# A spectral filter with a mixer on one core: first group of batch 0 closed by selection matmuls, and a new order of the opening loads

## The chip, the cores and the metric

The kernel runs on one core of a Trainium2 chip. The metric is the device time of one execution in microseconds. A core has five engines, each with its own queue that is worked in order: TensorE (PE in the profile; its weight loads are PEld), VectorE (DVE), ScalarE (ACT), GpSimd (POOL) and SyncE (SP). Transfers are issued by SP, by ScalarE and, where the type changes on the way, by GpSimd.

## The reference

```python
def _attn_ref(x, filt_r, filt_i):              # x: (8, 3136, 256)
    X = np.fft.rfft(x, axis=1)
    Y = X * (filt_r + 1j * filt_i)[None, :, :]
    return np.fft.irfft(Y, n=x.shape[1], axis=1).astype(np.float32)

def _moe_ref(x, U, V, w_ch1, w_ch2):           # U: (3136, 32), V: (32, 3136)
    h = x.transpose(0, 2, 1) @ U @ V
    u = x + h.transpose(0, 2, 1)
    ch = np.maximum(u @ w_ch1, 0.0) @ w_ch2    # 256 -> 1024 -> 256
    return (u + ch).astype(np.float32)
```

The second function is applied to the output of the first. All inputs and outputs are float32; the kernel computes in float16 with float32 sums.

## The kernel before

The sequence of 3136 is split as 64 x 49, and the transform is done by matmuls in four stages, for each of eight batches.

- Stage 1 (`st1`, lines 260 to 290): a transform over the 64, with its twiddle factors folded into the matrix `wf`. Thirteen units per batch; the result goes to a DRAM scratch, `ct1`. Batch 0 takes another way: `turned` (line 295) gives the result turned round, and it stays on chip (`cm`, which lies in the tile `fc`).
- Stage 2 and the filter: a transform over the 49 (`stage2`, matmuls of lines 348 to 352), and a product with the filter. For batch 0 (`mid_first`, line 354) half a block at a time is multiplied once (L400 on VectorE, L397 on GpSimd after a copy by ScalarE, L395), with four stage-2 matmuls for a block of two halves and four in stage 3. For later batches (`plan_mid`, line 610) a block of four frequencies has two stage-2 matmuls (`two`), three products (`mul`, L628, L630, L632, on VectorE, or on GpSimd for the blocks that are `pooled`) and a sum on GpSimd (L634). These need turned and negated copies of the filter tiles, which `make_fa` (line 541) makes: L543 on ScalarE, L544 and L545 on VectorE.
- Stage 3 (`stage3`, L344): back over the 49; the result is copied to `esb` (L326) and stored to a second DRAM scratch, `ct2` (L329). `low_rank` (L416) and `low_rank_end` (L424, L426) take the product with U from the same tiles.
- Groups. Each batch's output is made in six groups of 512 tokens and a small one of 128 for two batches together. `load_e2` (L438, by SP) brings a group's 64 rows from `ct2`, `put_h` adds 32 rows for the low-rank part, and `stage4` (L477, copied to `ut` by L482) is the transform back over the 64 with the matrix `sv`, whose last 32 rows are V. Then `mm1` (L488) and its relu (L492) make one of eight parts of the hidden layer; this is a step. `mm2_part` (L521) of the group before, with `residual` (L497), runs in the same step, and the result leaves by L529 and L536.

The order of instructions on every engine is the order in which the program writes them. The opening is written out (lines 552 to 578): `u_hat`, `turned`, `mid_first`, stage 1 of batch 1, then stage 4 of the first group. After it, a loop over groups and steps issues what two lists hold for each step: `early` ahead of mm1 and `plan` behind mm2. `plan_mid`, `plan_st1` and `plan_rest` fill them, so that stages 1 to 3 of batch b run in the steps of batch b-1 (and stage 1 of b+1 before them). Each instruction waits for its data by semaphores, with all behind it in its queue. GpSimd is not tied to the steps: it goes on as soon as the data of its next instruction are there. `load_x` (two issues per tile, L170) uses four tile buffers; the tile rings and PSUM banks (`bank`) set further waits.

## Time and profile before

| | |
|---|---|
| median of 6 runs | 556.64 us (555.33 to 559.0) |
| the profiled execution's own time | 555.66 us |
| its span | 553.9 us |
| mean granted TensorE clock | 0.986 |
| busy: PE, ACT, DVE, POOL | 517.1, 390.9, 352.9, 282.4 us |
| first mm1 (L488) | 57.33 us |
| last store issued (L513) | 550.09 us |

The page lists busy time by engine, then the span in 40 slices of 13.8 us with the busy share in tenths, the granted clock and the DMA load. Other views of the same execution give the busy time of each engine in a chosen stretch, what each engine waited for in a stretch, and single instructions in order of time. Times are from the start of the span. A wait is put down to what came last.

### The profile page before, as it was taken

The numbers are of one execution on the slowest core, as the hardware profiler recorded it, in microseconds if no ns is written. First come the engines' busy times: TensorE is split into PE (matmuls) and PEld (weight loads), VectorE is DVE, ScalarE is ACT, GpSimd is POOL, SyncE is SP. The second block draws the span as 40 slices with busy tenths as digits, with TensorE's granted clock in tenths as the row PEclk, the third lists the DMA queues.
The fourth block names the chain that finished last, engine by engine and source line by source line (L and its number), as shares of the span: only waits on it lengthen the run. The fifth ranks groups of instructions, "written<-read, shape, count | busy, mean of one in ns | idle before, by whom it ended". The sixth has DMA issues, their size and how long they took to land.

```text
span 553.9 us, 11638 instructions
## 1 busy us (share of the span) xinstructions
PE 517.1 (93%) x4491; PEld 375.4 (68%) x4491; DVE 352.9 (64%) x409; ACT 390.9 (71%) x684; POOL 282.4 (51%) x194
## 2 busy tenths in 40 slices
PE   5986698987999999999999999999999999999996
PEld 3733366764767777677776777777776777777775
DVE  6774864754746785758746785768646887643332
ACT  8576778764777688677777788668767677765663
POOL 5787379931893165815683185807563287300000
PEclk9999799997999999999999999999999999999999
DMA  9998888885669468775879469865654554333212
GB/s 196 160 177 184 227 172 212 184 198 158 164 175 252 129 172 209 161 200 145 196 213 219 123 173 234 168 201 152 178 171 126 141 164 121 106 113 115 96 78 87
DMA packets 85433, 92.06 MB, mean 166 GB/s; under 512 B 6742, under 2 KB 69417, under 8 KB 85377
## 3 DMA queue, kind: packets, MB, share of 16 engines
q1 hardware_dynamic: 67968, 75.12, 45.6%
q0 software_dynamic: 16960, 15.91, 19.2%
q8 instruction: 35, 0.57, 0.4%
q10 hardware_dynamic: 448, 0.28, 0.2%
q14 instruction: 22, 0.17, 0.1%
HBM read 57.42 MB, written 49.77 MB: 194 GB/s over the span
## 4 chain that ended last, share of the span: by engine, by line
PE 64%; POOL 5%; DVE 3%; ACT 1%; issue 1%; DMA 1%; ACTq 0%; POOLq 0%; DVEq 0%
PE psum L521 24%; PE psum L488 23%; PE psum L352 3%; PE psum L344 3%; PE psum L497 3%; PE psum L477 3%; PE psum L266 2%; POOL y L634 2%; DVE tb L632 1%; PE psum L416 1%; POOL x L170 1%; POOL tb L632 1%; POOL tb L630 1%; POOL ta L628 1%; DVE ut L482 1%
## 5 line engine op out<-in xcount | busy, mean ns | idle before, releaser
L492 ACT ACTIVATE hring<-psum 128x512 f16<-128x512 f32 (+1 forms) x416 | 237.6, 576 | 103.7 <-PE psum L488 102.4
L488 PE MATMUL psum<-ut,w1sb 128*128 128x512 f16 (+1 forms) x832 | 241.7, 372 | 3.5 <-ACT hring L492 1.7
L521 PE MATMUL psum<-w2sb,hring 128*128 128x256 f16 x1536 | 231.4, 274 | 0.0
L634 POOL TENSOR_TENSOR y<-ta,tb 128x1024 f16<-128x1024 f16 x56 | 120.5, 2159 | 160.8 <-DVE tb L632 129.3
L521 PEld LDWEIGHTS <-hring 128*128 128x128 f16 x1536 | 143.7, 98 | 62.8 <-issue 3.0
L482 DVE CAST ut<-psum 128x512 f16<-128x512 f32 x96 | 71.0, 740 | 107.6 <-PE psum L477 86.3
L488 PEld LDWEIGHTS <-w1sb 128*128 128x128 f16 x832 | 104.8, 145 | 26.3 <-issue 9.5
L529 DVE COPY och<-psum 128x512 f32<-128x512 f32 x96 | 66.1, 689 | 47.6 <-PE psum L497 46.2
L326 ACT CAST esb<-psum 98x512 f16<-98x512 f32 x128 | 74.7, 586 | 20.4 <-PE psum L344 14.3
L628 DVE TENSOR_TENSOR ta<-psum,fb 128x1024 f16<-128x1024 f32 x41 | 49.9, 1218 | 9.5 <-PE psum L352 8.5
L273 ACT CAST asb<-psum 128x512 f16<-128x512 f32 x78 | 45.7, 589 | 14.3 <-PE psum L266 13.2
L497 PE MATMUL psum<-idn,ut 128*128 128x128 f16 x392 | 54.0, 219 | 0.0
L477 PEld LDWEIGHTS <-e 96*128 96x128 f16 x768 | 35.7, 98 | 25.2 <-issue 9.8
L630 DVE TENSOR_TENSOR tb<-psum,fc 64x1024 f16<-64x1024 f32 x41 | 50.3, 1226 | 0.9
L632 DVE TENSOR_TENSOR tb<-psum,fc 64x1024 f16<-64x1024 f32 x41 | 49.9, 1218 | 0.8
L477 PE MATMUL psum<-sv,e 96*128 96x64 f16 x768 | 38.6, 193 | 6.1 <-DMA e<-ct 3.4
L344 PE MATMUL psum<-y,g 128*98 128x512 f16 x105 | 40.1, 382 | 2.7 <-POOL y L634 1.3
L497 PEld LDWEIGHTS <-ut 128*128 128x128 f16 x392 | 38.5, 98 | 4.9
L352 PE MATMUL psum<-a,w2t 98*128 98x512 f16 x113 | 34.7, 383 | 4.6 <-DMA a<-ct 3.6
L628 POOL TENSOR_TENSOR ta<-pc,fb 128x1024 f16<-128x1024 f16 x15 | 32.4, 2158 | 11.8 <-ACT pc L638 11.8
L266 PE MATMUL psum<-x,wf 128*128 128x256 f16 x168 | 31.6, 275 | 3.2 <-DVE asb L271 1.0
L630 POOL TENSOR_TENSOR tb<-pc,fc 64x1024 f16<-64x1024 f16 x15 | 31.8, 2123 | 1.2
(93 smaller groups left out, 370.3 us busy)
## 6 DMA issues: line engine op xcount, KB each, us to landing
out_dram<-och SPq DMA_DIRECT2D x47, 512.0 KB
ct<-esb SPq DMA_DIRECT2D x64, 196.0 KB
x<-in_x_dram POOLq DMA_DIRECT2D x48, 256.0 KB, 8.3
e<-ct SPq DMA_DIRECT2D x48, 256.0 KB
a<-ct SPq DMA_DIRECT2D x56, 196.0 KB
ct<-asb SPq DMA_DIRECT2D x42, 256.0 KB
...
```

The source lines that it names most:

```text
L326: nc.scalar.copy(esb[b, k][:, 2 * half:2 * half + 2, :].rearrange("p s d -> p (s d)"), pe[0:98])
L477: nc.tensor.matmul(pu[:, 64 * i:64 * i + 64], e2[b, c][:, i, 128 * dh:128 * dh + 128], sv[:, 64 * r:64 * r + 64], start=(i == 0), stop=Tru ...
L482: nc.vector.tensor_copy(o, v)
L488: nc.tensor.matmul(ph[:, 0:n], w1sb[:, dh, :, t], gr.ut[:, dh, 0:n], start=(dh == 0), stop=(dh == 1))
L492: nc.scalar.activation(h[:, 0:n], ph[:, 0:n], RELU)
L497: nc.tensor.matmul(o[:, dh * 128:dh * 128 + 128], gr.ut[:, dh, t0:t0 + n], idn, start=False, stop=(dh == 1), skip_group_check=True)
L521: nc.tensor.matmul(o, gr.h[tt][:, i * 128:(i + 1) * 128], w2sb[:, tt, :], start=(tt == 0), stop=False, skip_group_check=True)
L529: nc.vector.tensor_copy(gr.och[:, 2 * y:2 * y + 2, :].rearrange("p j d -> p (j d)"), gr.pc)
L628: eng.tensor_mul(ta, p, va)
L630: eng.tensor_mul(tb[0:64], p[64:128], vb[64:128])
L632: eng.tensor_mul(tb[64:128], p[0:64], vb[0:64])
L634: nc.gpsimd.tensor_add(ys[k], ta, tb)
```

## The change

- The opening. `wf` is loaded at half its size and spread out by two products with a column of zeros and ones on VectorE; U comes in float32 by SP; `u_hat` is done in pieces between the calls of `turned`; `cm` has a tile of its own. The first part of `sv` and `kr` are loaded after batch 0's first block, the rest of `sv` after its last; the filter's last slot is loaded after `w1`.
- `mid_first`: two turned blocks instead of four ahead of the first stage 2; only product 13 is on GpSimd; the parts of the low-rank product follow their blocks. Stage 4 of the first group reads from DRAM only what the first six blocks stored. What the last two blocks add is picked out of `esb` by 0/1 matrices (`sel`, `pick`, 64 small matmuls), copied once (`zs`) and multiplied with `s4x`; the low-rank part is a third product into the same bank.
- Batch 1. Only x tile 0 is loaded early; the other loads and the second weight stand behind product 13 on GpSimd, and the second weight is read in pieces of 512 numbers. Three units of stage 1 come ahead of the first mm1, ten in steps 0 to 7; its last three stores go out on GpSimd, behind eight copies of filter tiles there. Four of its eight blocks (0, 1, 6, 7) are multiplied once per half, as batch 0's are, the others later than before (steps 17 to 37 for their stage 2).
- The turned and negated filter copies are made in 24 pieces: eight copies on GpSimd after the loads, eight negations and four copies on VectorE in steps 5 to 13, four copies on GpSimd late in batch 0.
- Loads of x: batch 2 in steps 13 to 16, behind a one-element copy on GpSimd that reads the first stage-1 block of batch 1; batch 3 in steps 47 to 53 instead of with stage 1 of batch 2.
- The plans of batches 2 and 3 begin later, batch 2 with three blocks on GpSimd instead of two. Tiles of 128 rows become 113 rows. From step 98 on the plan is as before.

The diff, cut to its core:

```diff
+    sel = np.zeros((98, 4, 60))
+    s4x = np.zeros((128, 512))
+    for g in range(4):
+        for h in range(2):
+            for c in range(2):
+                sel[49 * c + 2 * g + h, g, 28 + 2 * h + c] = 1.0
+                n = 64 * (2 * g + h)
+                s4x[32 * g + 2 * h + c:32 * g + 32:4, n:n + 64] = s[48 + c:64:2, 2 * g + h]
+    wf = np.concatenate([wf.reshape(128, 25 * 64).astype(f16), pair.view(f16)], axis=1)
...
-    wf = cst.tile([128, 25, 128], F16, name="wf")
-    for c in range(4):
-        i = slice(8 * c, min(8 * c + 8, 25))
-        nc.sync.dma_start(wf[:, i], wf_d.rearrange("p (i m) -> p i m", m=128)[:, i])
+
+    usb = hflat[0:64, 0:2 * NR * RANK].bitcast(F32)
+    nc.sync.dma_start(usb, moe_U.rearrange("(q r) p -> q (r p)", q=NQ))
+    wfc = hflat[:, 6272:6272 + 1604]
+    nc.sync.dma_start(wfc, wf_d)
+    wf = cst.tile([128, 24, 128], F16, name="wf")
+    wl = cst.tile([64, 64], F16, name="wl")
...
+    cm = cst.tile([128, 7232], F16, name="cm")
+    nc.vector.memset(cm[:, 2 * SEQ:], 0.0)
...
+    for h in range(2):
+        nc.vector.tensor_scalar_mul(wf[:, :, 64 * h:64 * h + 64],
+                                    wfc[:, 0:1536].rearrange("p (i m) -> p i m", m=64),
+                                    wfc[:, 1600 + 2 * h:1602 + 2 * h].bitcast(F32))
+    nc.vector.tensor_copy(wl, wfc[0:64, 1536:1600])
+    tbs = [cst.tile([NZ, 4 * DM], F16, name=f"tb_{i}") for i in range(3)]
+    for t in tbs:
+        nc.vector.memset(t[32:64], 0.0)
...
-    w2sb = cst.tile([128, 8, DM], F16, name="w2sb")
-    vnat = hflat[64:96, 4704:4704 + SEQ]
+    w2sb = cst.tile([128, 4, 2 * DM + 16], F16, name="w2sb")
...
                 dst = asb[:, 2 * j:2 * j + 2, :].rearrange("p i d -> p (i d)")
-                if b == 1 and j % 2:
-                    nc.vector.tensor_copy(dst, pf)
-                else:
-                    nc.scalar.copy(dst, pf)
+                (nc.vector.tensor_copy if 4 * c + j in by else nc.scalar.copy)(dst, pf)
                 if j < 3:
                     yield
             for h in range(2):
-                nc.sync.dma_start(dram(ct1[b], (16 * c + h) * 64 * DM,
-                                       [[DM, 64], [128 * DM, 8], [1, DM]]), asb[64 * h:64 * h + 64])
-            if 1 < b < NB - 1 and c:
+                (nc.gpsimd if (b, c) == (1, 2) else nc.sync).dma_start(
+                    dram(ct1[b], (16 * c + h) * 64 * DM, [[DM, 64], [128 * DM, 8], [1, DM]]),
+                    asb[64 * h:64 * h + 64])
+            if 2 < b < NB - 1 and c:
                 load_x(b + 1, c - 1)
...
+    def make_fc(k, copy):
+        copy(fc[0:NR, 4 * k:4 * k + 4], fb[64:NZ, 4 * k:4 * k + 4])
+
+    def make_neg(k):
+        nc.vector.tensor_scalar_mul(fc[64:NZ, 4 * k:4 * k + 4], fb[64:NZ, 4 * k:4 * k + 4], -1.0)
+
+    def make_fa(k, copy):
+        copy(fa[64:NZ, 4 * k:4 * k + 4], fb[0:NR, 4 * k:4 * k + 4])
+        if k == 7:
+            nc.gpsimd.tensor_copy(fa[64:65, 31, :], fc[0:1, 31, :])
+            for p in (0, 64):
+                nc.gpsimd.memset(fc[p:p + 1, 31, :], 0.0)
+
...
+        def low_rank_part(k):
+            for i in range(4):
+                a = 4 * k + i
+                nc.tensor.matmul(ph[32 * i:32 * i + 32], uh[:, a, :], esb[0, k][:, i, :],
+                                 start=(k == 0), stop=(k == 7), skip_group_check=True)
+
+        whole = []
+        pu = [psum[:, 2 + dh, :] for dh in range(2)]
+        zp = psum[:, 0, 0:DM]
+
+        def pick(j):
+
+            for i in range(2):
+                sl = 2 * (j - 12) + i
+                for g in range(4):
+                    nc.tensor.matmul(zp[32 * g:32 * g + 32], sel[:, g, 28 - 4 * sl:60 - 4 * sl],
+                                     esb[0, j // 2][:, 2 * (j % 2) + i, :], start=(sl == 0),
+                                     stop=(sl == 7), skip_group_check=True)
 
         def do3(j, uv):
             pe = bank("e0")
             stage3(pe, [(uv[:, 0], 2, 4), (uv[:, 1], 3, 5)], j == 15)
-            out3(0, j // 2, j % 2, pe)
-
-        for k in range(4):
+            while whole and j > 3:
+                low_rank_part(whole.pop(0))
+            if j > 13:
+                pick(j - 2)
+            k = j // 2
+            out3(0, k, j % 2, pe)
+            if ndone[0, k] == 2:
+                whole.append(k)
+                if k == 0:
+                    nc.sync.dma_start(sv[0:64, 0:512], s4_d[:, 0:512])
+                    nc.sync.dma_start(kr, kr_d)
+                if k == 5:
+                    load_e2(0, 0, 48)
+                if k == 6:
+                    load_e2(0, 1, 48)
+                if k == 7:
+                    load_e2(0, 1, 64, 48)
+                    nc.sync.dma_start(sv[0:64, 512:], s4_d[:, 512:])
+                    load_e2(0, 2)
+                    load_e2(0, 6)
...
+
+        for k in range(2):
             turn_a2(k)
-        for c in range(4):
-            load_x(1, c)
-        nc.gpsimd.dma_start(w2sb, moe_w_ch2.rearrange("(cc t) e -> cc (t e)", t=8))
+        load_x(1, 0)
+        nc.gpsimd.tensor_copy(sv[64:96, :].rearrange("p (r q) -> p r q", q=NQ),
+                              vnat.rearrange("p (q r) -> p r q", q=64))
...
-            if j in (7, 9, 12, 14):
-                pc = sb.tile([128, 2, 2 * DM], F16, tag="pc", bufs=2, name="pc")
-                nc.scalar.copy(pc, pz)
-                uv = sb.tile([128, 2, 2 * DM], F16, tag="y", bufs=3, name="uv")
+            fin = free(fb, 0, NZ, 2 * j * DM, [[0, 2], [1, 2 * DM]])
+            uv = sb.tile([NZ, 2, 2 * DM], F16, tag="y" if j == 13 else "ta", bufs=3, name="uv")
+            if j == 13:
+                pc = sb.tile([NZ, 2, 2 * DM], F16, tag="pc", bufs=2, name="pc")
+                nc.scalar.copy(pc, pz[0:NZ])
                 nc.gpsimd.tensor_mul(uv, pc, fin)
             else:
-                uv = sb.tile([128, 2, 2 * DM], F16, tag="ta", bufs=3, name="uv")
-                nc.vector.tensor_mul(uv, pz, fin)
-            if j < 4:
-                turn_a2(j + 4)
+                nc.vector.tensor_mul(uv, pz[0:NZ], fin)
+            if j < 6:
+                turn_a2(j + 2)
             todo.append((j, uv))
-            if len(todo) > 3:
+            if j == 15:
+                todo = [todo[i] for i in (1, 0, 2)]
+            while len(todo) > 2 or todo and j == 15:
                 do3(*todo.pop(0))
-        while todo:
-            do3(*todo.pop(0))
-
-
-    h1 = {}
+        step1(1)
+        step1(1)
+        pick(14)
+        low_rank_part(7)
+        pick(15)
+        h1[0] = hp = sb.tile([128, DM], F16, tag="hp", bufs=1, name="hp")
+        nc.vector.tensor_copy(hp, ph)
+        zs = sb.tile([128, DM], F16, tag="zs", bufs=1, name="zs")
+        nc.scalar.copy(zs, zp)
+        keep_warm(2, psum[:, 7, :])
+        low_rank_end(0)
+        gr = groups[0]
+        gr.ut = sb.tile([128, 2, 512], F16, tag="ut", bufs=3, name="ut")
+        for dh in range(2):
+            for i in range(8):
+                nc.tensor.matmul(pu[dh][:, 64 * i:64 * i + 64],
+                                 e2[0, 0][0:48, i, 128 * dh:128 * dh + 128],
+                                 sv[0:48, 64 * i:64 * i + 64], start=(i == 0), stop=False,
+                                 skip_group_check=True)
+        for dh in range(2):
+            nc.tensor.matmul(pu[dh], zs[:, 128 * dh:128 * dh + 128], s4x, start=False, stop=False,
+                             skip_group_check=True)
+        step1(1)
+        for dh in range(2):
+            nc.tensor.matmul(pu[dh], h1[0][64:96, 128 * dh:128 * dh + 128], sv[64:96, 0:512],
+                             start=False, stop=True, skip_group_check=True)
+            (nc.scalar.copy if dh else nc.vector.tensor_copy)(
+                gr.ut[:, dh, :].rearrange("p (j q s) -> p s j q", q=64, s=2),
+                pu[dh].rearrange("p (s j q) -> p s j q", s=2, q=64))
...
     keep_warm(10)
-    u_hat()
-    for c in range(4):
-        turned(c)
-        keep_warm(2)
-    nc.sync.dma_start(sv[0:64], s4_d)
-    nc.sync.dma_start(kr, kr_d)
+    turned(0, 0)
+    u_hat(0, 8)
+    keep_warm(2)
+    turned(0, 1)
+    u_hat(16)
+    keep_warm(2)
+    for c in (2, 3):
+        turned(0, c)
+    u_hat(24)
+    gens, a2q = {}, {}
+
+    def step1(b):
+        if b not in gens:
+            gens[b] = st1(b, (0, 3, 4, 5, 7, 8, 9, 11) if b == 1 else ())
+        next(gens[b])
+
     mid_first()
-    load_e2(0, 0)
-    load_e2(0, 1)
-    nc.gpsimd.tensor_copy(sv[64:96, :].rearrange("p (r q) -> p r q", q=NQ),
-                          vnat.rearrange("p (q r) -> p r q", q=64))
-    low_rank(0)
-    for n, _ in enumerate(st1(1)):
-        if n == 3:
-            low_rank_end(0)
-        if n == 6:
-            put_h(0, 0)
-    load_e2(0, 2)
-    load_e2(0, 6)
-    keep_warm(6)
-    stage4(groups[0], 0)
-    stage4(groups[0], 1)
-    for c in (1, 2, 6):
-        put_h(0, c)
-    make_fa(0)
-    make_fa(1)
+    keep_warm(3, psum[:, 7, :])
+    load_x(1, 1)
+    load_x(1, 3)
+    load_x(1, 2)
+    nc.gpsimd.dma_start(w2sb[:, :, 0:2 * DM], moe_w_ch2.rearrange("(cc i t) e -> cc i (t e)", i=4, t=2))
+    for k in (3, 2, 5, 4, 0, 1, 6, 7):
+        make_fc(k, nc.gpsimd.tensor_copy)
+    put_h(0, 1)
...
+        def two_q(k, half):
+            box[k, half] = [psum[:, 5:7, :]]
+            for f in range(2):
+                stage2(psum[:, 5 + f], w2t[:, 128 * f:128 * f + 128],
+                       w2t[:, 256 + 128 * f:384 + 128 * f],
+                       a2[k][:, 2 * half * DM:2 * half * DM + 2 * DM], (k, half) == (7, 1))
+
+        def mul_q(k, half):
+            uv = sb.tile([NZ, 2, 2 * DM], F16, tag="ta", bufs=3, name="uv")
+            nc.vector.tensor_mul(uv, box[k, half][0][0:NZ],
+                                 free(fb, 0, NZ, (4 * k + 2 * half) * DM, [[0, 2], [1, 2 * DM]]))
+            box[k, half].append(uv)
+
+        def three_q(k, half):
+            uv = box[k, half][1]
+            pe = bank("e")
+            stage3(pe, [(uv[:, 0], 2, 4), (uv[:, 1], 3, 5)], (k, half) == (7, 1))
+            out3(b, k, half, pe)
+
+        end = 0
+        if b == 1:
+
+            for k, q in ((0, 11), (3, 11), (1, 11), (5, 11), (2, 17), (4, 20), (6, 22), (7, 25)):
+                at(q, fetch, k)
+            for k, q, d in ((3, 17, 26), (5, 21, 31), (2, 23, 33), (4, 28, 37)):
+                at(q, two, k)
+                if k % 2:
+                    early[q + 1].append((pooled, (k,)))
+                else:
+                    w = q
+                    for i in range(3):
+                        w += 1
+                        while not ok_dve(w):
+                            w += 1
+                        early[w].append((mul, (k, i, nc.vector)))
+                for half in range(2):
+                    at(d + half, three, k, half)
+            for k, qs in ((0, (15, 16)), (1, (19, 20)), (6, (33, 34)), (7, (36, 37))):
+                for half, q in enumerate(qs):
+                    at(q, two_q, k, half)
+                    early[q + 1].append((mul_q, (k, half)))
+                    at(q + (3 if k == 7 else 2), three_q, k, half)
+            return 40
...
         for k in range(3):
-            at(later(s, -lead), fetch, k)
-        end = 0
+            at(later(s, -5 if b == 2 else -9), fetch, k)
         for k in range(8):
...
-                s = later(s, 3 if b > 1 else 1)
+                s = later(s, 3)
...
-                d = max(later(s, 5), end)
+                d = max(later(s, 3 if (b, k) == (2, 7) else 5), end)
...
     for c in range(3, 6):
         at(8 * c - 14, load_e2, 0, c)
-    at(1, make_fa, 2)
-    at(3, make_fa, 3)
-
-    def x_after(b):
-
-        for c in range(4):
-            load_x(b, c, groups[0].h[3] if c == 0 else None)
-
-    at(4, x_after, 2)
+    for n, c in ((7, 2), (8, 6), (9, 0)):
+        at(n, put_h, 0, c)
+    for n in (0, 0, 1, 1, 2, 3, 4, 5, 6, 7):
+        at(n, step1, 1)
+    at(13, lambda: load_x(2, 0, a2q[0][0:1, 0:1]))
+    for c in range(4):
+        if c:
+            at(13 + c, load_x, 2, c)
+        at((47, 49, 51, 53)[c], load_x, 3, c)
+    for n, k in ((5, 0), (5, 1), (7, 2), (8, 3), (8, 4), (9, 5), (11, 6), (11, 7)):
+        at(n, make_neg, k)
+    for n, k in ((12, 2), (12, 3), (13, 4), (13, 5)):
+        at(n, make_fa, k, nc.vector.tensor_copy)
+    for n, k in ((34, 0), (35, 1), (40, 6), (41, 7)):
+        at(n, make_fa, k, nc.gpsimd.tensor_copy)
     for b in range(1, NB):
         if b == 2:
-            plan_st1(b, 12, (0, 1, 3, 4, 5, 7))
+            plan_st1(b, 18, (0, 3, 4, 5, 7))
         elif b > 2:
-            plan_st1(b, later(start[b - 1], -60))
-        m = later(start[b - 1], (5, -9, -12)[min(b, 3) - 1])
-        z = plan_mid(b, m, (2, 5) if b > 1 else (1, 3, 5))
+            plan_st1(b, later(start[b - 1], -46 if b == 3 else -60), (0, 3, 4, 5, 7) if b == 3 else (0, 4, 7))
+        m = later(start[b - 1], (16, -4, -12)[min(b, 3) - 1])
+        z = plan_mid(b, m, (2, 5) if b > 2 else (1, 3, 5))
...
                 f(*a)
             mm1(gr, t)
-            if n + 1 < len(groups) and t in ((2, 6) if n != 5 else (6, 7)):
-                stage4(groups[n + 1], t // 4 if n != 5 else t - 6)
+            turns = {0: (5, 6), 5: (6, 7)}.get(n, (2, 6))
+            if n + 1 < len(groups) and t in turns:
```

## The prediction

> **What bounds the kernel now.** I read the busy rows and slices of the page first, then the busy time by stretch, then TensorE's waits by window, then single rows in time order. A "step" is one mm1 (line 488) with its relu (L492). The relu rows in time order put step 0 at 58.7, 16 at 80.6, 40 at 116.6, 48 at 133.3 and 98 at 190.6 us; each step's number and work follow from the plan lists.
>
> The page:
>
> ```profile
> PE 517.1 (93%) x4491; PEld 375.4 (68%) x4491; DVE 352.9 (64%) x409; ACT 390.9 (71%) x684; POOL 282.4 (51%) x194
> PE   5986698987999999999999999999999999999996
> PEclk9999799997999999999999999999999999999999
> ```
>
> TensorE is the bound from slice 10 on. The first ten slices hold nearly all that is lost, and the two low clock digits lie there. By stretch (PE, PEld, DVE, ACT, POOL, clock, DMA share, GB/s):
>
> ```profile
> 46.00:57.30 11.30, 6.96 (x80) 4.50 (x80) 5.70 (x8) 7.73 (x13) 5.94 (x1) 1.00 0.73 191
> 60.20:63.60 3.40, 1.54 (x6) 0.68 (x6) 3.01 (x6) 3.40 (x4) 0.65 (x2) 1.00 0.68 175
> 63.60:70.50 6.90, 5.14 (x22) 2.54 (x22) 6.14 (x10) 3.50 (x6) 4.31 (x7) 0.51 0.94 214
> ...
> 125.10:128.50 3.40, 0.72 (x13) 0.71 (x14) 0.22 (x1) 0.00 (x0) 0.00 (x0) 1.00 0.82 222
> 128.50:135.30 6.80, 5.96 (x31) 3.54 (x29) 4.94 (x6) 2.52 (x5) 1.57 (x1) 0.50 0.43 128
> ```
>
> Two thin stretches, each followed by 6.8 us at half clock. TensorE's waits from 57 to 75 us and from 110 to 140 us name the causes:
>
> ```profile
> PE psum L352 <- DMA a<-ct: 2.2, 1, 2.2
> PE psum L488 <- ACT hring L492: 1.7, 2, 1.5
> ```
> ```profile
> PE psum L477 <- DMA e<-ct: 3.4, 1, 3.4
> PE psum L352 <- DMA a<-ct: 1.4, 1, 1.4
> ```
>
> The last is the hand-off to batch 1: its final ct store is issued at 117.80, its e load only at 123.88, and stage 4 starts at 127.78. The rows that price the opening:
>
> ```profile
> 24.79 3.48 DVE L400 TENSOR_TENSOR uv<-psum,fb 128x1024 f16<-128x1024 f32 x3
> 41.16 5.85 SPq L329 DMA_DIRECT2D ct<-esb  x4
> 44.98 6.96 POOL L562 COPY sv<-hring 32x3136 f16<-32x3136 f16 x1
> 52.09 1.10 SPq L438 DMA_DIRECT2D e<-ct  x2
> ```
>
> Products of batch 0 start at 24.79, its last ct store is issued near 47.0, the e loads wait for it until 52.09, and the first mm1 comes at 57.33.
>
> **The change, stage by stage.** From step 98 on both plans are the same, so all is decided before 190.6.
>
> *A, up to the first mm1 (57.3 before).* The DMA share is 1.03 in the first 20 us, at 194 GB/s, and the x landings pace the four turned(c), at 13.55, 16.0, 18.7 and 20.4. Ahead of them half of wf (-399 KB) and sv with kr (-416 KB) go away; U in f32 and sel with s4x come in (+196, +174). Net -445 KB, at 194 GB/s 2.3 us. The expansion of wf and the f32 U copies (DVE, some 3 us, by L243's 1.48 and L544's 0.69 for 2048) hide under x. Two turn-backs instead of four before the first stage 2 give 0.5 more: first product at 22.0. The loop is DVE's: 15 products x 1.23 + one copy 0.69 = 19.1, to 41.1 (before 12 on DVE with 4 on GpSimd: also 19.1). Last esb 43.5, against 46.7.
>
> Then the gain: before, 10.7 us of store, load and stage 4 follow. After, columns 0 to 47 of group 0 need only ct stores 0 to 5, and the rest comes from the selection matmuls (64 of L416's form, 0.03 each, 2.0 in all, three of four picks between waits for esb). esb 11 is done at 39.8; store to landing 2.4 (180.53 to 182.89), load 3.1 (62.28 to 65.36): e at 45.3; sixteen matmuls 0.4, s4x 0.43, a stage-1 unit 0.22, h part 0.2, ut 0.74: first mm1 at 47.3. The other branch (hp 0.37, kr 0.27, h1 0.36, h part, ut, from 43.8) ends at 46.3 and is covered. **A: -10.0.** If store and load take what they take before (5.1 and 3.9), 50.8.
>
> *B, first mm1 to step 16 (23.3 before).* make_fa leaves ScalarE (L543, four of 1.89) and becomes eight GpSimd copies of 49x1024, with negs and copies on DVE at 0.35 each (half of L544's 0.69). Ten stage-1 units (0.22 on TensorE each, 2.1 in all; copies 0.58 to 0.69, eight of twelve on DVE) enter steps 0 to 7. Moved behind GpSimd's product (41.8): five x(1) issues at 0.65 and w2sb 0.57, so issued by 45.8; then the copies; then three ct_1 stores, which a(1,0) on SP needs. Some 2 MB of x, w2sb and e take 10.5 us at 190 GB/s; the 2 KB pieces I cost at nothing, as w2 is due only at step 8. Stage 4 of group 1 at step 5 needs sv's rest and e_1, near 52.5 (store of k=7 at 44, landed 47 to 48, then loads): about 1 us of wait. Step 8 at 56.5; seven steps at 1.05: step 15 ends at 64. asb of c=2 is ready at 57.2, stores 1.3, landing 3.5, load 3.1: a(1,0) at 65.2, wait 1.2; step 16 at 66.7. x(2) waits on GpSimd behind a(1,0), and behind it queue batch 1's pooled products; stage 1 of batch 2 begins at step 19, 5 us later, so it is just covered. **B: 19.4, -3.9.**
>
> That holds while GpSimd is free by 57.2, at up to 1.43 us per copy. The trace has one copy on GpSimd: L562, 3136 elements with a strided input in 6.96, so 2.2 ns each, 2.3 per copy and 18.2 for eight. The Trainium skill, "GPSIMD Engine Reference", section 4.1 with 3.1, says two inputs cost twice VectorE but one input runs at about line rate (1.03 cycles of 1.2 GHz per element): an estimate of 0.88 per copy, 7 for eight; it also calls GpSimd the wrong engine for plain elementwise work. By the row GpSimd is free at 64.0, by the page at 52.8. The trace agrees for two inputs (L634 2.1 ns per element); a contiguous single input is not in it. The row's input is strided, so I take 1.2 (9.6), nearer the page; both ends stay in the range.
>
> The wait at step 5 could also drop the clock. "TensorE: Matmul & The Clock Gate" (HAM oscillation) speaks of idle gaps over about 3.4 us. The trace is harsher: 1.54 busy in 3.40 was enough at 60.2, with a longest gap of 2.2. By the page a 1 us wait costs nothing more; by the row a thin stretch costs 3.4 (half of 6.8). At 52 the neighbours are busy some 65%, so I charge none here.
>
> *C, steps 16 to 40 (36.0 before).* TensorE content from spacings of starts (mm1 pair 0.43, four mm2 0.43, residual pair 0.11, stage 4 0.21, stage-2 pair 0.43, stage-3 half 0.21, stage-1 unit 0.22): before 20.6+1.3+1.3+2.0+2.6+2.9 = 30.7, so 5.3 of waits, with GpSimd busy 37.25 of 38 us from 72 to 110. After: 20.6+1.3+1.3+2.9+3.0+1.7+3.4+1.7 = 35.9, as four blocks of batch 1 use four matmuls for two; GpSimd falls to about 26 of 38 and I leave half the waits. **C: 38.5, +2.5.**
>
> *D, steps 40 to 48 (16.7 before).* Content 9.7. The chain from the last stage 3 to stage 4 at step 46: esb 0.6, issue 0.3, store 2.4 to 6.1, load 3.1 to 3.9, thus 6.4 to 10.9 against 7.3 of steps. x of batch 3 has later steps, but GpSimd is not held by steps: its first half tile goes once the fa copies are through, near step 40, and three a(2) loads stand ahead of the store on SP. So I take 9.5, a wait of 2.2, and half of a 3.4 clock loss: **D: 13.7, -3.0.**
>
> *E, steps 48 to 98 (57.3 before).* One stage-2 block and four stage-1 units fewer are behind us: 0.43+0.88, rounded to **+1.5**. Batch 2 now ends at step 92 for stage 4 at 98, 7.8 us: just enough for 6.4 to 7.
>
> Sum: -10.0-3.9+2.5-3.0+1.5 = **-12.9**: span 541.0 for 553.9. The profiled run took 555.66, 1.8 over its span; the median is 556.64. So **543.7**.
>
> **The rivals.**
> - *No stall at all* (0.19): A's other branch sets mm1 (-1), no wait for a(1,0) (-1.2), D at its content plus 0.5 (-3.5): 538. For it: from 140 to 300 us TensorE's waits add up to only 1.9 us. Against: by the bytes counted in B the DMA engines stay near full until past 60 us.
> - *The first group is not closed sooner than its e load* (0.09): store 5.1, load 3.9 as before: mm1 at 50.8, 547.2. For it: rows 41.16 and 52.09; against: x(1) is no longer in flight at 40.
> - *GpSimd copies at the strided row's 2.3* (0.11): a(1,0) at 71.9, 6.7 later, and a half-clock spell 3.4: 553.8.
> - *Slower* (0.08): the same queue at over 2.6 us per copy. It decides when 8 x (c - 1.43) and the 3.4 exceed 12.9: from c = 2.6 us; at 3.2 it gives 561. For it: DVE's copies and negs run beside these on the same tiles; against: no GpSimd group with two inputs has a mean over 2.16.
> - *Gains and losses cancel* (0.03), 555 to 558.
>
> **How the numbers follow.** The forecast has 0.50, its own range 540 to 548. 0.3% (1.7 us) is what a measurement tells from no change. Faster: 0.50+0.19+0.09+0.11 = 0.89; same 0.03; slower 0.08. The range for 8 in 10 runs from 535, below the no-stall case, to 553: a tenth or so is left above and less below.
>
> **What would show it.** First mm1 near 47; a wait of TensorE for e or sv near step 5 of about 1 us; GpSimd's eight copies at 1.2 each, ending by 56; a<-ct waited for little at step 15; step 16 at 66.7, 40 at 105, 48 at 119, 98 at 178; one half-clock spell instead of two. It is wrong if the copies take over 1.5 us, if mm1 comes after 50, or if a wait for e<-ct near steps 46 or 98 exceeds 3.4.

## The result, and the profile after

The changed kernel takes **558.14 us** (median of 35 runs, 555.47 to 561.36) against 556.17 for the kernel before in the same session (72 runs): ratio 1.0035, 95% interval 1.0021 to 1.0049. It is slower by a third of a per cent, where 543.7 was forecast. The profiled execution took 558.06 us, its span is 556.2 (before: 553.9).

By the stages of the forecast (relu rows in time order, both traces):

| stage | before | after | moved by | forecast |
|---|---|---|---|---|
| A, to the first mm1 | 57.3 | 50.0 | -7.3 | -10.0 |
| B, first mm1 to step 16 | 23.3 | 22.6 | -0.7 | -3.9 |
| C, steps 16 to 40 | 36.0 | 39.9 | +3.9 | +2.5 |
| D, steps 40 to 48 | 16.7 | 18.6 | +1.9 | -3.0 |
| E, steps 48 to 98 | 57.3 | 60.5 | +3.2 | +1.5 |
| F, step 98 to the end | 363.3 | 364.6 | +1.3 | 0 |
| span | 553.9 | 556.2 | +2.3 | -12.9 |

The 15.2 us between forecast and trace (14.4 between the medians) are therefore 2.7 in A, 3.2 in B, 1.4 in C, 4.9 in D, 1.7 in E and 1.3 in F. The page of the changed kernel, busy time and slices:

```profile
PE 521.3 (94%) x4540; PEld 374.3 (67%) x4540; DVE 352.6 (63%) x413; ACT 375.0 (67%) x678; POOL 283.9 (51%) x204
PE   5898789968998999999999999999999999999996
PEclk9898989998999999999999999999999999999999
```

The low clock digits are more and shallower: where the kernel before had two spells of some 6.8 us at half clock, there are now two of 3.4 us and one of 6.8 from 40 us on, and one of 3.4 at 20.2. Busy time by stretch (PE, PEld, DVE, ACT, POOL, clock, DMA share, GB/s) shows the three from 40 us on, each behind the stretch of 3.4 us that came before it:

```profile
44.10:47.50 3.40, 1.36 (x22) 0.83 (x20) 0.42 (x1) 0.00 (x0) 3.36 (x5) 1.00 1.20 259
47.50:50.90 3.40, 3.40 (x11) 0.97 (x9) 1.52 (x2) 1.31 (x2) 3.40 (x4) 0.50 1.19 223
68.00:71.40 3.40, 0.81 (x8) 0.55 (x6) 1.25 (x2) 0.54 (x1) 0.18 (x1) 1.00 0.55 174
71.40:74.80 3.40, 3.40 (x12) 1.57 (x11) 1.69 (x2) 0.60 (x1) 3.15 (x6) 0.50 0.90 249
119.20:122.60 3.40, 1.38 (x10) 0.94 (x10) 1.01 (x2) 0.25 (x1) 0.00 (x0) 1.00 0.72 218
122.60:129.40 6.80, 4.06 (x30) 2.28 (x29) 2.82 (x4) 1.50 (x3) 0.00 (x0) 0.50 0.66 149
```

What TensorE waited for, from 20 to 75 us and then from 110 to 140 us:

```profile
PE psum L399 <- DMA a<-ct: 2.6, 1, 2.6
PE psum L516 <- DMA e<-ct: 2.0, 1, 2.0
PE psum L598 <- DMA sv<-s: 1.7, 1, 1.7
```
```profile
PE psum L399 <- DMA a<-ct: 3.0, 1, 3.0
PE psum L598 <- DMA e<-ct: 2.7, 1, 2.7
```

Here `a` is a block of stage 1's result, loaded back from `ct1`; a(1,0) is the first of batch 1. `e` is a group's rows from `ct2`; e_1 is that of group 1. Every long wait is for a DMA that SP issues. The rows of SP and of GpSimd, in order of time, say why (start, duration, what was issued):

```profile
38.86 0.31 SPq L376 DMA_DIRECT2D ct<-esb  x1
41.25 0.32 SPq L558 DMA_DIRECT2D e<-ct  x1
...
42.76 0.63 SPq L376 DMA_DIRECT2D ct<-esb  x1
52.95 0.32 SPq L558 DMA_DIRECT2D e<-ct  x1
53.31 0.45 SPq L470 DMA_DIRECT2D sv<-s  x1
...
115.31 0.43 SPq L376 DMA_DIRECT2D ct<-esb  x1
122.86 0.49 SPq L558 DMA_DIRECT2D e<-ct  x1
```
```profile
40.57 1.30 POOL L187 DMA_DIRECT2D x<-in_x_dram  x2
...
42.39 1.28 POOL L187 DMA_DIRECT2D x<-in_x_dram  x2
43.63 0.76 POOL L683 DMA_DIRECT2D w2sb<-in_moe_w_ch_dram  x1
44.43 8.39 POOL L405 COPY fc<-fb 49x1024 f16<-49x1024 f16 x8
...
112.28 1.30 POOL L187 DMA_DIRECT2D x<-in_x_dram  x2
```

The load behind a ct store waits until that store has landed, so the gap between the two issues measures the landing. (The load behind block 7's store takes rows of block 6 too, whose store was issued 0.9 us earlier.) The store of block 5 needs 2.4 us (38.86 to 41.25), as forecast. The store of block 7, issued while the second of two x tiles was being started and 0.9 us ahead of the second weight, needs 10.2 us. Batch 1's last store, three us behind the first x load of batch 3, needs 7.5 us. In the kernel before the same store needed 6.1:

```profile
117.80 0.31 SPq L329 DMA_DIRECT2D ct<-esb  x1
123.88 0.51 SPq L438 DMA_DIRECT2D e<-ct  x1
```

There GpSimd had started its last x load some ten us ahead of it (four from 105.66 on, 5.4 to 12.6 us to landing).

### The profile page after: what moved, and what is told of

Read it like the earlier page. It is cut to its first block, busy times and chain, and to the rows that moved or that the text cites. A ratio compares the mean times of both kernels' runs of the same rounds, so it can differ in the third digit from the quotient of the medians.

```text
span 556.2 us, 11732 instructions
## 1 busy us (share of the span) xinstructions
PE 521.3 (94%) x4540; PEld 374.3 (67%) x4540; DVE 352.6 (63%) x413; ACT 375.0 (67%) x678; POOL 283.9 (51%) x204
## 4 chain that ended last, share of the span: by engine, by line
PE 55%; POOL 5%; DVE 1%; ACT 1%; issue 1%; DMA 1%; ACTq 0%; POOLq 0%
PE psum L642 21%; PE psum L609 21%; PE psum L618 3%; PE psum L598 3%; PE psum L399 3%; PE psum L391 2%; PE psum L304 2%; POOL y L743 2%; POOL x L187 1%; PE psum L536 1%; POOL ta L737 1%; POOL tb L741 1%; POOL tb L739 1%; DMA a<-ct 1%; DVE ut L603 0%
## 5 line engine op out<-in xcount | busy, mean ns | idle before, releaser
L743 POOL TENSOR_TENSOR y<-ta,tb 113x1024 f16<-113x1024 f16 x52 | 112.5, 2169 | 154.3 <-DVE tb L741 117.8
L603 DVE CAST ut<-psum 128x512 f16<-128x512 f32 x94 | 69.5, 740 | 99.4 <-PE psum L598 81.1
L308 ACT CAST asb<-psum 128x512 f16<-128x512 f32 x76 | 44.9, 590 | 14.9 <-PE psum L304 13.7
L598 PEld LDWEIGHTS <-e 96*128 96x128 f16 x752 | 34.9, 98 | 25.4 <-issue 10.5
L737 DVE TENSOR_TENSOR ta<-psum,fb 113x1024 f16<-113x1024 f32 x37 | 45.1, 1218 | 10.4 <-PE psum L399 6.8
L399 PE MATMUL psum<-a,w2t 98*128 98x512 f16 x120 | 37.7, 392 | 8.9 <-DMA a<-ct 5.6
L739 DVE TENSOR_TENSOR tb<-psum,fc 49x1024 f16<-49x1024 f32 x37 | 45.4, 1226 | 1.0
L741 DVE TENSOR_TENSOR tb<-psum,fc 49x1024 f16<-49x1024 f32 x37 | 45.1, 1218 | 1.0
L391 PE MATMUL psum<-y,g 113*98 113x512 f16 x98 | 37.4, 381 | 2.9 <-POOL y L743 1.6
L737 POOL TENSOR_TENSOR ta<-pc,fb 113x1024 f16<-113x1024 f16 x15 | 32.4, 2158 | 11.3 <-ACT pc L747 11.2
L739 POOL TENSOR_TENSOR tb<-pc,fc 49x1024 f16<-49x1024 f16 x15 | 31.8, 2121 | 1.2
```

The source lines that it names most:

```text
L399: nc.tensor.matmul(pz, w, a, start=True, stop=True)
L598: nc.tensor.matmul(pu[:, 64 * i:64 * i + 64], e2[b, c][:, i, 128 * dh:128 * dh + 128], sv[:, 64 * r:64 * r + 64], start=(i == 0), stop=Tru ...
L603: (nc.scalar.copy if gr is groups[0] and dh else nc.vector.tensor_copy)(o, v)
L737: eng.tensor_mul(ta, p[0:NZ], va)
L739: eng.tensor_mul(tb[0:NR], p[64:NZ], vb[64:NZ])
L743: nc.gpsimd.tensor_add(ys[k], ta, tb)
```

## The experiments

Three theories were put to the test. LOADS: transfers that GpSimd starts (x, the second weight) lengthen whatever SP has under way, and its chains of store and load are what TensorE waits for. WORK: what was moved into the steps costs TensorE as much as the opening gained. X3: the load of x of batch 3 spoils the hand-off to batch 1. Steps are given as in the table above; ratios are to the kernel before, measured beside each run. The changed kernel's own ratio is 1.0035.

### e1: x of batch 1 and the second weight back ahead of the first product

```diff
         load_x(1, 0)
+        load_x(1, 1); load_x(1, 3); load_x(1, 2)
+        nc.gpsimd.dma_start(w2sb[...], moe_w_ch2...)
         nc.gpsimd.tensor_copy(sv[64:96, :]...)
```

> Three theories on why 7.3 us of an earlier first step are gone by the end. LOADS: the x tiles of batch 1 and the second weight, moved to 40-46 us, are in flight just when SP's short chain (store of blocks 5 to 7, loads of e and sv) needs the DMA engines, and the third of these stores takes 9.5 us to land. WORK: the opening's gain is real, but the ten stage-1 units and sixteen stage-2 and stage-3 matmuls that were put into steps 0 to 40 eat it, whatever the transfers do. X3: the load of x of batch 3, which GpSimd starts at 112.3, and the a loads hold back batch 1's last ct_1 store (7.5 us). Here the five loads go back to where they were issued before, ahead of the first product. LOADS: the last store of batch 0 lands in 3 to 4 us (by 47), first step's mm1 near 48, no wait for sv at step 5, step 16 at 68 to 69 (72.6 in the changed kernel), total 553 to 555. WORK: first mm1 at 48 to 50, step 40 within 1.5 us of the 112.5 of the changed kernel, total 557 to 559. X3: as WORK, with the hand-off at steps 40 to 48 still 18 us.

Measured: 559.94 us, ratio 1.0074 (1.0050 to 1.0097). Slower than the changed kernel. SP's and GpSimd's rows:

```profile
48.74 0.42 SPq L376 DMA_DIRECT2D ct<-esb  x1
52.38 0.32 SPq L562 DMA_DIRECT2D e<-ct  x1
```
```profile
31.42 1.22 POOL L187 DMA_DIRECT2D x<-in_x_dram  x2 [4.14 <-PE psum L391]
...
35.20 6.91 POOL L481 COPY sv<-hring 32x3136 f16<-32x3136 f16 x1
42.20 2.11 POOL L495 TENSOR_TENSOR uv<-pc,fb 113x1024 f16<-113x1024 f16 x1
```

With nothing of GpSimd's in flight (the second weight, its last load, landed at 47.1) the store of block 7 lands in 3.6 us, as LOADS says. But the loads waited 4.1 us and held up the sv copy, and that held up GpSimd's one product (42.2 for 38.5), for which TensorE waited 3.8 us; the first mm1 came 5 us later. The edit mixed two things.

### e2: x of batch 3 held to step 47

```diff
-        at((47, 49, 51, 53)[c], load_x, 3, c)
+        at((47, ...)[c], lambda c=c: load_x(3, c, groups[5].h[7][0:1, 0:1] if c == 0 else None))
```

> The first x load of batch 3 is held on GpSimd until the relu of step 47 by a one-element copy that reads it, so that it goes at about 131 us and not at 112.3. X3: the last ct_1 store lands in 3 to 4 us instead of 7.5, steps 40 to 48 take 14 to 15 us instead of 18.6, the half-clock spell of 6.8 us at 122.6 goes or halves, total 553 to 555. LOADS or WORK: the store still takes over 6 us because the a loads ahead of it are in the way, steps 40 to 48 stay at 17.5 to 19, total 557 to 559.

Measured: **552.96 us, ratio 0.9940 (0.9917 to 0.9963)**. One line makes the change a gain. SP's rows:

```profile
115.01 0.38 SPq L376 DMA_DIRECT2D ct<-esb  x1
118.58 0.49 SPq L558 DMA_DIRECT2D e<-ct  x1
```

The store lands in 3.6 us instead of 7.5; TensorE no longer waits for a (3.0), and the half-clock spell is 3.4 instead of 6.8 us:

```profile
122.00:125.40 3.40, 3.25 (x26) 2.29 (x27) 2.58 (x3) 0.60 (x1) 0.18 (x1) 0.50 0.82 172
```

Steps 40 to 48 take 14.9 us for 18.6. X3 holds, and is LOADS in another place. All later kernels except e3 and e4 have this edit. In the thirteen traces that have it these steps take 13.0 to 15.1 us, in the four without it (changed kernel, e1, e3, e4) 18.2 to 19.1.

### e3: the first group closed the ordinary way

```diff
-                if k == 5: load_e2(0, 0, 48)
                 if k == 7:
+                    load_e2(0, 0)
...
-        pick(14) ... pick(15); zs; the s4x products
+        put_h(0, 0); stage4(groups[0], 0); stage4(groups[0], 1)
```

> The changed kernel without the selection: the first group waits for the store of the last block and a full e load, and the low-rank rows are put beside it as before; the 64 selection matmuls are gone. What is asked is whether an earlier first step reaches the end at all. First mm1 at 57 to 59 by every theory (the last store lands at 52.9, then the load and stage 4). If the opening's gain is carried (WORK, X3): the total grows by the same 7 to 9 us, to 565 to 567. If batch 1's own chain of loads and stores sets the pace (LOADS): stage 1 of batch 1 still runs at its own data's times, step 16 moves by 3 us or less, total 558 to 562.

Measured: 564.12 us, ratio 1.0141 (1.0118 to 1.0163): 1.06% or 5.9 us more than the changed kernel. Step 0 is at 59.3 for 51.1, step 16 at 79.2 for 72.6. The total lies between the two forecasts, but step 16 moved by 6.6 us where LOADS allowed 3, and from there to step 98 every stage is as long as in the changed kernel to within 0.4 us (steps 16 to 24: 15.97 us in both). So the opening's gain is carried to the end; it is not swallowed by a later chain. What ate it is a loss of its own.

### e4: x tiles 1 to 3 of batch 1 not loaded

```diff
-    load_x(1, 1); load_x(1, 3); load_x(1, 2)
+    xt[1, 1], xt[1, 2], xt[1, 3] = xt[0, 1], xt[0, 2], xt[0, 3]
```

> The x tiles 1 to 3 of batch 1 are not loaded at all; its stage 1 reads batch 0's tiles, so batch 1 is computed from wrong data. The second weight is loaded as in the changed kernel. This leaves 1.6 MB less of reads in the stretch from 40 to 53 us. LOADS: the last ct store of batch 0 lands within 4 us, e within 3.3, first mm1 at 47.5 to 48.5, sv and e_1 in time for step 5, step 16 at 67 to 69, total 552 to 555. WORK or X3: first mm1 may gain 1 to 2 us, step 40 moves by less than 1.5 us, total 556.5 to 559.

Measured: 555.23 us, ratio 0.9986 (0.9963 to 1.0010), 0.5% or 2.7 us less than the changed kernel; step 16 at 70.4 for 72.6. LOADS had the sign, but only half the size: with the weight alone in flight the store of block 7 still takes 6.4 us.

```profile
41.87 0.55 SPq L376 DMA_DIRECT2D ct<-esb  x1
48.31 0.32 SPq L558 DMA_DIRECT2D e<-ct  x1
```

### e5, e9: x of batch 1 into the gap after the sv copy, or spread

From 36 to 40 us the DMA engines of the changed kernel are at 0.28. e5 puts both x tiles there; e9 puts tile 1 there, tile 2 behind the third GpSimd copy and the weight behind the seventh.

```diff
         nc.gpsimd.tensor_copy(sv[64:96, :]...)
+        load_x(1, 1); load_x(1, 3)          # e5: load_x(1, 2) too
...
     for k in (3, 2, 5, 4, 0, 1, 6, 7):
         make_fc(k, nc.gpsimd.tensor_copy)
+        if k == 5: load_x(1, 2)             # e9
+        if k == 6: nc.gpsimd.dma_start(w2sb[...], ...)
```

> On top of the kernel with x of batch 3 held (552.96). Putting the five loads ahead of the sv copy made GpSimd late for its product (42.2 instead of 38.5), so that run mixed two things. Here x tiles 1 to 3 of batch 1 stand right behind the sv copy: GpSimd has nothing to do from 34.6 to 38.5 and the DMA engines are at 0.28 from 36 to 40. The second weight stays behind the product. LOADS: x is through by about 46, the store of the last block lands in 4 to 6 us instead of 9.5, no wait for sv at step 5, first mm1 49 to 50.5, step 16 at 69 to 70.5 instead of 72.0, total 550 to 551.5. WORK: step 16 at 71 to 72.5 (the wait moves on to a(1,0) at step 15), total 552 to 554; slower than 555 if the store of block 5 at 39 now lands later and the first mm1 comes after 52.

> On top of the kernel with x of batch 3 held. The runs before showed that a store of SP lands in 2.4 us when no x tile is in flight and in 6 to 9.5 when one is, wherever the x loads stand; so what counts is what is in flight at 39 to 42 (store of block 5, load of e) and at 43 to 46 (store of block 7). Here x tile 1 of batch 1 goes behind the sv copy (35), tile 2 behind the third of the eight GpSimd copies (near 44), the second weight behind the seventh (near 50). LOADS: tile 1 is nearly through by 41, so the store of block 5 lands in 3 to 4 us and first mm1 comes at 50 to 51.5; the store of block 7 lands in 4 to 6 us (47 to 49), the wait for sv goes; step 16 at 70 to 71; total 549.5 to 551.5. If instead tile 1 at 35 to 41 costs the first group 4 us as the two tiles did, first mm1 is at 53 to 54 and the total 555 to 557.

Measured: e5 557.54 us, ratio 1.0015 (0.9993 to 1.0037), worse than e2; e9 553.68 us, ratio 0.9949 (0.9923 to 0.9975), no different from e2. SP's rows of e5:

```profile
39.22 0.31 SPq L376 DMA_DIRECT2D ct<-esb  x1
45.09 0.32 SPq L561 DMA_DIRECT2D e<-ct  x1
...
46.39 0.42 SPq L376 DMA_DIRECT2D ct<-esb  x1
50.77 0.32 SPq L561 DMA_DIRECT2D e<-ct  x1
```

Now it is the store of block 5 that takes 5.9 us (4.8 in e9), while block 7's takes 4.4 (6.6 in e9, with one x tile just started). Step 0 falls back to 54.9 in e5. The delay went to whichever store was issued while x was in flight. So the loads' place in the changed kernel, behind the product, is right for the first group, and its price is the second group's wait for sv.

### e6, e8: the second weight later, or in one piece

```diff
-    nc.gpsimd.dma_start(w2sb[...], ...)                 # e6: moved behind the eight make_fc
-    w2sb = cst.tile([128, 4, 2 * DM + 16], ...)         # e8
+    w2sb = cst.tile([128, 4, 2 * DM], ...)
```

> On top of the kernel with x of batch 3 held (552.96). Only the second weight moves, from 43.6 us to behind the eight GpSimd copies (issued near 52); x of batch 1 stays at 40.6. It is due at step 8, at 60.5. LOADS: 1 MB less of reads before 52, so the last store of batch 0 lands 2 to 4 us sooner, the wait for sv at step 5 (1.4) goes, and if the weight lands by 60 step 16 comes at 70 to 71, total 551 to 552. If it lands later, TensorE waits for it at step 8 by 1 to 4 us and the total is 553 to 556. WORK: no change of more than 1 us.

> On top of the kernel with x of batch 3 held (552.96). The second weight is read again as one piece of 2048 numbers per partition instead of four pieces of 512: the tile loses the 16 numbers between its pieces. If the size of the pieces matters, the stores and loads that run beside it from 43.6 on land at other times: sooner with small pieces by LOADS, so here the sv wait at step 5 grows from 1.4 to 2.5 or more and the total by 1 to 2. If it doesn't, as the forecast had it (costed at nothing), every step stays within 0.5 us and the total at 552 to 554.

Measured: e6 553.30 us, ratio 0.9914 (0.9891 to 0.9938); e8 555.43 us, ratio 0.9959 (0.9934 to 0.9983). Neither differs from e2 by more than the intervals. In e6 block 7's store still takes 9.0 us, with x alone in flight:

```profile
43.00 0.49 SPq L376 DMA_DIRECT2D ct<-esb  x1
52.03 0.32 SPq L558 DMA_DIRECT2D e<-ct  x1
```

In e8 it takes 10.9 and every step from 16 on is within 0.6 us of e2's. The size of the pieces makes no difference that can be seen here.

### e7: sixteen matmuls of batch 1 left out

```diff
-            for f in range(2):                           # two_q
+            for f in range(1):
-            stage3(pe, [(uv[:, 0], 2, 4), (uv[:, 1], 3, 5)], ...)
+            stage3(pe, [(uv[:, 0], 2, 4)], ...)
```

> On top of the kernel with x of batch 3 held (552.96). In the four blocks of batch 1 that are multiplied once per half, the second of the two stage-2 matmuls and the second of the stage-3 pairs are left out, so batch 1 is computed wrongly; 8 stage-2 and 8 or 9 stage-3 matmuls of 512 columns go, the products and stores stay. WORK: steps 16 to 40 are limited by TensorE's own content and shrink by 16 x 0.215 = 3.4 us, from 39.8 to 36.4, total 549 to 550. If another engine (GpSimd, busy 13.4 of 16 us in steps 16 to 24) sets the pace there: steps 16 to 40 shrink by less than 1 us, total 552 to 553.5.

Measured: 553.50 us, ratio 0.9968 (0.9940 to 0.9996), no gain over e2. Busy time by stretch, steps 16 to 24 and 32 to 40, of e7 and then of e2:

```profile
69.80:86.10 16.30, 12.38 (x95) 8.37 (x93) 7.70 (x9) 10.24 (x18) 14.61 (x12) 1.00 0.98 210
96.90:108.50 11.60, 11.54 (x92) 7.86 (x90) 8.74 (x10) 10.26 (x21) 7.08 (x8) 1.00 0.56 158
```
```profile
72.00:88.00 16.00, 14.98 (x103) 9.63 (x102) 7.29 (x9) 10.38 (x19) 13.39 (x11) 0.93 0.97 197
98.70:111.80 13.10, 13.04 (x99) 8.69 (x97) 8.87 (x10) 10.57 (x21) 7.16 (x8) 1.00 0.53 150
```

In steps 32 to 40 the stretch shrinks by 1.5 us, seven matmuls of 0.215: there TensorE's content is the bound, as WORK says. (The other sixteen traces, of the changed kernel and its variants, all have 13.2 us for these steps.) In steps 16 to 24 about as many went and nothing was gained; the wait that took their place, in TensorE's waits of that stretch:

```profile
PE psum L304 <- DMA x<-in_x_dram: 2.5, 1, 2.5
```

There x of batch 2 comes just behind; its loads wait on GpSimd for a(1,0). In the changed kernel itself TensorE does not wait for it in these steps.

### e12: x of batch 2 not held back (on e6)

```diff
-    at(13, lambda: load_x(2, 0, a2q[0][0:1, 0:1]))
+    at(13, lambda: load_x(2, 0))
```

> On top of the kernel with x of batch 3 held and the second weight late. The one-element copy that holds the x loads of batch 2 back until a(1,0) has landed (71) is left out, so that they go right behind the last ct_1 stores, near 64. If x in flight lengthens whatever SP waits for (LOADS): the last ct_1 store lands at 69 to 72 instead of 68, a(1,0) 2 to 4 us later, step 16 at 73 to 75, total up by 2 to 3 us. If steps 16 to 24 wait for x of batch 2 (a wait of 2.5 us for it showed once sixteen matmuls were gone): steps 16 to 24 take 15 us or less instead of 16, total the same or down by 1.

Measured: 559.82 us, ratio 1.0047 (1.0024 to 1.0070), against 0.9914 for e6: about 7 us lost. GpSimd starts x at 63.21, right behind the last ct_1 stores; TensorE's wait for a(1,0), 1.7 us in e6, becomes

```profile
PE psum L399 <- DMA a<-ct: 4.7, 1, 4.7
```

and a spell of 6.8 us at half clock begins at 73.1 (another, at 127.7, lies at the hand-off to batch 1). The stores ahead of it land as in e6: the a loads are issued at 67.40 for 67.45. It is the load of a(1,0) that now takes 6.4 us for 2.8. This is LOADS at a third place, in a load instead of a store, and with the sign turned round: here the change's own hold is what keeps it away.

### e10, e11: two smaller orders on SP (on e6)

```diff
-            at(later(s, -5 if b == 2 else -9), fetch, k)                          # e10
+            at(later(s, (-5 if k == 0 else -1) if b == 2 else -9), fetch, k)
-                (nc.gpsimd if (b, c) == (1, 2) else nc.sync).dma_start(           # e11, al too
+                nc.sync.dma_start(
```

> On top of the kernel with x of batch 3 held and the second weight late (553.3; ratio to the kernel before 0.991). Of the three a loads of batch 2 that stand ahead of batch 1's last ct store on SP, two (0.4 MB) go four steps later, behind the e loads. LOADS: the store, issued at 115 before, is issued 0.8 us sooner and lands in 2.6 to 3 us instead of 3.6; steps 40 to 48 take 13 to 14 us instead of 15; total 1 to 2 us less than that kernel. WORK: TensorE has 9.7 us of content in these steps and the rest is the chain of stage 3, copy, store, load, stage 4, whatever else is in flight: less than 0.5 us.

> On top of the kernel with x of batch 3 held and the second weight late. The last three stores of stage 1 of batch 1 are issued by SP, as before the change, and not by GpSimd. They were issued at 61.7 to 64 on GpSimd, a(1,0) came at 71, and TensorE waited 1.7 us for it at step 15. If GpSimd's slower issue or its queue is part of that: a(1,0) comes 1 to 2 us sooner, step 16 at 70, total 1 us less. If the step in which stage 1's last unit runs sets it (its copy ends at 61.3 in either): step 16 moves by less than 0.5 us. If the stores now hold back SP's e loads behind them: slower by 1 us or more.

Measured: e10 552.96 us, ratio 0.9939 (0.9913 to 0.9964); e11 553.45 us, ratio 0.9945 (0.9920 to 0.9969). Neither is faster than e6. In their profiles each does what it should: e10's last store lands in 3.1 us and steps 40 to 48 take 13.2 us for 15.1; in e11 the wait for a(1,0) is 1.1 us and steps 0 to 16 take 18.6 us for 20.6. The totals don't show it. In e10 steps 16 to 24 took 18.6 us, with 3.0 of waits for x of batch 2.

### e13, e14: four edits together, and two GpSimd blocks in batch 2

e13 is e2, e9, e10 and e11 in one. e14 adds:

```diff
-        z = plan_mid(b, m, (2, 5) if b > 2 else (1, 3, 5))
+        z = plan_mid(b, m, (2, 5) if b > 1 else (1, 3, 5))
```

> Four edits together: x of batch 3 held to step 47; x tile 1 of batch 1 behind the sv copy, tile 2 and the second weight spread between the GpSimd copies; batch 1's last ct_1 stores on SP; two of the three a loads of batch 2 behind the e loads. If the losses are landing times that each depend on what is in flight just then (LOADS), they add up: opening as in the spread kernel (step 0 at 51.4), step 16 some 1.5 us sooner than its 70.8 by the wait for a(1,0), steps 40 to 48 13 us instead of 14.5, total 547.5 to 550, a ratio to the kernel before of 0.985 to 0.990. If what is won at one wait comes back at the next (x of batch 2 in steps 16 to 24, TensorE's content), total 551 to 554, ratio 0.991 to 0.996, no better than the single edits.

> The four edits together, and batch 2 with two blocks on GpSimd (2 and 5) as before the change instead of three (1, 3 and 5). In steps 56 to 80 GpSimd is busy 27.7 of 28.2 us. If GpSimd sets the pace there: steps 48 to 98 take 58 to 59 us instead of 61 and the total falls by 2 to 3. If TensorE's content does (27.3 busy of the same 28.2): less than 0.5 us either way; VectorE has three products more and can make it up to 1 us slower.

Measured: e13 551.95 us, ratio 0.9904 (0.9871 to 0.9938); e14 551.46 us, ratio 0.9892 (0.9846 to 0.9939). The gains add up in part only: in e13 the first mm1 was early (step 0 at 48.3), and TensorE then waited 4.5 us for sv at step 5. Busy time by stretch, steps 56 to 64 and 64 to 80, of e13 and then of e14:

```profile
134.50:146.50 12.00, 11.30 (x94) 8.05 (x92) 6.81 (x9) 9.82 (x19) 11.79 (x9) 1.00 0.92 220
146.50:162.70 16.20, 15.99 (x148) 12.44 (x147) 6.67 (x9) 11.92 (x27) 15.90 (x10) 1.00 0.90 229
```
```profile
136.80:147.70 10.90, 10.53 (x89) 7.50 (x87) 7.35 (x8) 8.25 (x16) 10.68 (x7) 1.00 0.67 198
147.70:164.60 16.90, 16.69 (x153) 12.86 (x151) 7.13 (x10) 12.91 (x29) 13.96 (x11) 1.00 0.95 230
```

GpSimd has 3.0 us less to do (24.65 for 27.68 busy), the stretch is 0.4 shorter, and TensorE is busy 27.2 us in both. GpSimd looked full but is not the bound there.

### e15, e16: sv's load ahead of the stores it does not need (on e2, on e13)

```diff
+                if k == 3: nc.sync.dma_start(sv[0:64, 512:], s4_d[:, 512:])
                 if k == 7:
                     load_e2(0, 1, 64, 48)
-                    nc.sync.dma_start(sv[0:64, 512:], s4_d[:, 512:])
```

> On top of the kernel with x of batch 3 held (552.96; ratio to the kernel before 0.994). The load of sv's last 2624 columns (336 KB) needs no store, but stands on SP behind a load of e that waits for the store of block 7, so it is issued at 53.3 only. Here it goes after block 3, near 34 to 36, when the DMA engines are at 0.1 to 0.5. If SP's order is part of the loss: block 7's store still lands at 51 to 53 (x in flight), but only 16 rows of e are left to come after it; the wait at step 5 (1.4) falls to 0.5 or less, step 8 comes 1 to 1.5 us sooner (59 to 59.5), and with 336 KB less from 53 on c=2's stores and a(1,0) do too: step 16 at 69.5 to 71 for 72.0, total 550.5 to 552, ratio 0.989 to 0.992. If the landing times alone count (LOADS): the wait stays over 1 us, total as without the edit.

> The four edits together (551.95; ratio 0.990) and sv's rest after block 3. There TensorE waited 4.5 us for sv at step 5, since the x tile and the weight between the copies kept block 7's store until 51.5. If SP's order is part of the loss: that wait falls to 1.5 us or less and is named e, not sv; step 8 at 59 to 60 instead of 62, total 548 to 550, ratio 0.983 to 0.987. If what is won comes back at the next wait (a(1,0) at step 15): step 16 within 1 us of 70.8, total 551 to 553.

Measured: e15 553.73 us, ratio 0.9946 (0.9924 to 0.9968); e16 550.68 us, ratio 0.9898 (0.9858 to 0.9938). SP's rows of e15:

```profile
41.83 0.42 SPq L376 DMA_DIRECT2D ct<-esb  x1
52.06 0.81 SPq L559 DMA_DIRECT2D e<-ct  x2
```

Block 7's store still takes 10.2 us, yet the wait at step 5 is gone in e15 (1.4 us before) and down to 0.2 us in e16 (4.5 before), and steps 5 to 8 take 3.6 us in e15 for 5.2 in e2. So SP's order was part of that wait. The totals move by less than their intervals.

e13, e14 and e16 are all about 1% faster than the kernel before and, by the ratios, 1.3 to 1.4% faster than the changed one. Which of them is best can't be told.

## Why the prediction was wrong

- **A** (-7.3 for -10.0). Most was right: x turned at 10.0 to 15.3, the first product at 20.4 (22.0 forecast), the store of block 5 landed in 2.4 us. That the products ended at 41.0, as forecast, is partly luck: they began 1.6 us sooner and took 20.6 us for 19.1, with the half-clock spell of 20.2 to 23.6 among them. The step that failed is "load 3.1 (62.28 to 65.36): e at 45.3". The load was issued at 41.25, 0.7 us after x of batch 1, and TensorE got e at 46.33: 5.1 us. With the weight but no x in flight it is 4.3 (e4, 40.37 to 44.69), with neither at most 3.0 (e1, 47.45 to 50.47). The wait of 2.0 us left 3.4 us with TensorE busy 1.36, and the half-clock spell after it stretched the last 2.0 us of work to 3.6, three matmuls that only keep the clock up among them (L265, 48.71 on). The rival with mm1 at 50.8 was set aside because "x(1) is no longer in flight at 40"; x(1) starts at 40.57, and the forecast's own times (x issued from 41.8, the load from 42.2 to 45.3) had the two side by side.
- **B** (-0.7 for -3.9). GpSimd's copies were right: 1.05 us each for 1.2, near the 0.88 worked out from the Trainium skill ("GPSIMD Engine Reference", 4.1 with 3.1) and far from the strided row's 2.3. All rivals built on slow copies fell. What failed is "store of k=7 at 44, landed 47 to 48": issued 42.76, followed by its load only at 52.95. sv and e_1 came at 57.3 for 52.5, the c=2 store was issued at 62.9, its tile forecast for 57.2, and the wait for a(1,0) was 2.6 for 1.2, with a half-clock spell behind it. (The forecast's issues from 41.8 on also sum to 45.6, not 45.8, which changes nothing.) The forecast had counted the bytes (2 MB, 10.5 us) but applied them to the end of the transfers only, not to SP's stores among them.
- **C** (+3.9 for +2.5). The content was sized rightly: the matmuls of the trace at the forecast's prices give 35.6 us for its 35.9, and e7 confirms 0.215 us a matmul in steps 32 to 40. x of batch 2, called "just covered", was: TensorE does not wait for it there. The term that failed is "I leave half the waits": 2.6 us, where 4.3 of the 39.9 are not content. Only 1.0 of them is in waits that the trace names. The half-clock spell of 71.4 to 74.8 is not the rest: e8, e9, e11, e14 and e16 have the full clock in steps 16 to 24 and take 15.7 us for 16.0, and steps 24 to 40 take 23.9 us in all traces but e7's. Where the rest goes stays open.
- **D** (+1.9 for -3.0), the largest miss. The forecast saw that GpSimd would start x of batch 3 near step 40 and that three a loads stand ahead of the store, and priced both within "store 2.4 to 6.1", "a wait of 2.2". Measured: 7.5 us for the store, waits of 3.0 and 2.7, a full spell of 6.8 at half clock. e2 takes the x load away and gets 14.9 us, 1.2 from the forecast's 13.7. The price of a landing was read from the range of the kernel before, but the change started an x load three us ahead of the store, where the kernel before had started its last one some ten us ahead.
- **E and F** (+3.2 and +1.3 for +1.5 and 0). 2.7 of E's 3.2 us arise in steps 80 to 98, where the end of batch 2's plan now stands. The forecast counted only content there and put waits at nothing; the trace has 2.2 us of waits, the kernel before 0.4. The two longest are for a product on VectorE and for a sum on GpSimd:

```profile
PE psum L399 <- DVE tb L741: 1.0, 1, 1.0
PE psum L391 <- POOL y L743: 0.9, 1, 0.9
```

  No run took them away. e14 has both at the same length, and 21.9 us for these steps as the changed kernel has, so GpSimd's third block is not what lengthens them. In F, 1.0 us arises in steps 98 to 104; both plans are the same there, and its cause stays open.
- **The slower rival** got its chance of 0.08 for another mechanism. The one that happened, GpSimd's transfers lengthening what SP has under way, was touched only by the rival with mm1 at 50.8, for the first group alone, though each of its parts was in the text. With x of batch 1 absent the total falls by 2.7 us (e4), with x of batch 3 held by 5.3 (e2, four runs, by the ratios; the two spans differ by 3.6). If these two added up, it would be 8 of the 14.4 us between forecast and result; that sum wasn't run, and in e13 such gains added up in part only. The other 6 us are not shown to have this cause.
